# Giving back the slots of z earlier, and making the second mixing's pieces later

## The chip, the cores and the metric

The kernel runs on one core of one Trainium2 chip. The metric is the device time of one execution in microseconds, as a median of several runs; lower is better. Times inside an execution come from one profiled execution, counted from the start of its span. TensorE (PE in the rows; PEld is its weight load) multiplies into banks of PSUM, VectorE (DVE) and ScalarE (ACT) do the elementwise work, GpSimd (POOL) does small arithmetic and issues stores, and SyncE (SP) issues nearly all loads. Each of these works through its own queue in order.

## The reference

The program applies four layers to x, a float32 array of 2048 rows by 512 columns. Layers 0 and 2 mix, layers 1 and 3 are a gated feed-forward with 1792 hidden columns; the weights of the two of each kind are the same.

```python
def _A_ref(x, dft_seq_re, dft_seq_im, dft_hid_re, dft_hid_im):
    a = jnp.einsum("bsd,ed->bse", x, dft_hid_re)
    b = jnp.einsum("bsd,ed->bse", x, dft_hid_im)
    return jnp.einsum("ts,bse->bte", dft_seq_re, a) - jnp.einsum("ts,bse->bte", dft_seq_im, b)

def _B_ref(x, w_gate, w_up, w_down):
    return (_gelu(x @ w_gate) * (x @ w_up)) @ w_down

x = x + _A_ref(_layernorm(x), ...)
x = x + _B_ref(_layernorm(x), ...)
x = x + _A_ref(_layernorm(x), ...)
x = x + _B_ref(_layernorm(x), ...)
```

## The kernel before

**Numbers.** Every float32 operand is split into a high part (a rounding copy on ScalarE, L156) and a low part (a subtraction on VectorE, L158). A product is then three matmuls, high x high, high x low and low x high (`mm3`, L213 to L215), each 128x128 by 128x512. All of TensorE's real work runs through these three lines.

**Seven products in place of eight.** Both kinds of layer cut their matrix products into 2x2 blocks and use a scheme with seven block products. The names are those of the blocks of the weight and of the other operand: A11 with B11, A12 with B21, S1 with T1, S2 with T2, S3 with T3, S4 with B22, A22 with T4. S and T are sums and differences of blocks.

**Slots.** On-chip tiles of 128x512 float32 come from 98 numbered slots. `sb.get` takes the first number from the list of free ones, `sb.put` appends to its end, so the list is first in, first out. A slot may be handed out, in the program's text, while an earlier instruction that reads it has not yet run; the instruction that writes it next then waits for that reader. Which slot a load gets therefore decides what it waits for. The framework puts the instructions of each engine in order with a planning model of its own, so loads that have a free slot can be queued ahead of loads that stand earlier in the program's text.

**A feed-forward half.** `geglu(w, layer)` handles half w (1024 rows) of layer 1 or 3. Its normed rows, called z, lie transposed and split in `blocks`: 7 names x 2 chunks of 128, each a high and a low slot. Fourteen passes `up(n)`, n from 0 to 13, make the hidden values. Each pass runs the seven block products of `product(n, ps, an, bn, ...)` in this order: S2, S1, the next pass's A11 (`first(n + 1)`), S3, S4, the next pass's A12 (`second(n + 1)`), A22. A weight piece is given back behind its product, and the same piece for pass n + 2 is loaded from DRAM (`wb`, L1235). Even passes are followed by the gelu (L1245), odd ones by the multiplication with the gelu's result (L1261). The z blocks are read in all fourteen passes; they are given back in one loop behind the last (L1588).

**Beside the passes.** The down projection uses the same scheme over pairs of hidden blocks. Its A11 and A12 products run beside the passes (`beside`, one of six matmuls in each pass from n = 1); the other five names run behind the passes as a list of late products. Their weight pieces (`wc`) come through one stream of loads, issued on SP some items ahead (`take`, `load_next`, L333). In the second half of layer 1 the queue of steps also loads x again and makes the norm's terms for the next mixing (L241, L614 to L619, L640).

**The list `spare`.** In the second half of layer 1 (w = 1) a list of small jobs is laid out at L1386 to L1391. Four jobs make pieces of the hidden weights for two blocks of the second mixing: load a raw block (L1155 to L1157), four sums on VectorE, seven splits or half splits, and stores to DRAM (`wq`, L1182 and L1185, from POOL). Two jobs make summed blocks of the sequence weights: four loads (L1206), four sums, four stores (`ws`, L1216). Ahead of each job's work stands the load of the next one, and between them LET empty entries. `beside_mix(n)` takes one entry from the list each time it is called, which is six times in a pass, five of them through `beside_next`. It begins at pass n = 1 in layer 1. What the jobs make is read in layer 2, by SP loads from 1047 us on for `wq`. In layer 3 the same list holds products left over from layer 2, and is taken from in every pass.

Of the kernel before, what the change touches and what calls it, by code (L numbers as in the profile page):

```python
# [18 lines left out]
NF = F // P  # L19
# [24 lines left out]
MIXED = 4  # L44
PAIRED = {2: (2, 3)}
LATER = 3
LET = 5
SUMMED = 2
DOWN_RUNS = ((0,0,0,0),(4,4,4,0),(4,4,4,0),2)

# [2 lines left out]
def fnet_geglu(ctx: ExitStack, tc: tile.TileContext, x_in, ws, wh, wgu, wdn, wdc, whc, out):  # L53
# [86 lines left out]
    sb = Slots(slots, "s", NSLOT)  # L140
# [70 lines left out]
    def mm3(ps, a, b, start, stop):  # L211
        (ah, al), (bh, bl) = a, b
        nc.tensor.matmul(ps, ah, bh, start=start, stop=False, skip_group_check=True)  # L213
        nc.tensor.matmul(ps, ah, bl, start=False, stop=False, skip_group_check=True)  # L214
        newest["PE"] = nc.tensor.matmul(ps, al, bh, start=False, stop=stop, skip_group_check=True)  # L215
# [349 lines left out]
    def step():  # L565
        if queue:
            run = queue.pop(0)
            if run is not None:
                run()
        steps_done[0] += 1  # L570
        if slow and steps_done[0] % pace[0] == 0:
            slow.pop(0)()
# [129 lines left out]
    blocks = {}  # L702
# [98 lines left out]
    spare = []  # L801
# [429 lines left out]
    def piece_load(n, i):  # L1231
        tiles = [sb.get(F32R) for _ in range(2 if i < 3 else 1)]
        for k, t in enumerate(tiles):
            at = i * 1024 + k * 512
            nc.sync.dma_start(f32(t), wblocks[n][:, at:at + 512])  # L1235
        piece_here(n, i, tiles)
# [13 lines left out]
    def geglu(w, layer):  # L1250
# [43 lines left out]
        def product(n, ps, an, bn, start, stop):  # L1294
            step()
            hi, lo = wparts[n][an]
            for c in range(2):
                cut = slice(c * P, (c + 1) * P)
                mm3(ps, (hi[:, cut], lo[:, cut]), blocks[bn, c], start and c == 0, stop and c == 1)
            if an in ends:  # L1300
                i = ends[an]
                sb.put(*wparts[n][i])
                if not making and n + 2 < NF:
                    piece_load(n + 2, i)

        def first(n):
            if n < NF:
                chain[n] = ps8.get()
                product(n, chain[n], "A11", "B11", True, True)
                c11[n] = ps8.get()  # L1310
                seed(c11[n], chain[n])

        def second(n):
            if n < NF:
                ps = c11.pop(n)
                product(n, ps, "A12", "B21", False, True)
                finished(n, 0, 0, ps)
                ps8.put(ps)

        def beside_mix(n):  # L1320
            run = spare.pop(0) if spare and (layer > 1 or n >= 1) else None
            if run:
                run()

        def beside_next(n, down):
            beside_mix(n)
            next(down, None)

        def up(n):
# [4 lines left out]
            if n > 2 or w:  # L1334
                for _ in range(DOWN_RUNS[3]):
                    run = down_making.pop(0) if down_making else None
                    if run:
                        run()
            product(n, chain[n], "S2", "T2", False, True)
            u[n] = copied(chain[n])  # L1340
            down = beside(n)
# [4 lines left out]
            beside_next(n, down)  # L1346
            first(n + 1)
            beside_mix(n)
            product(n, chain[n], "S3", "T3", False, True)
            v = w4.pop(n)  # L1350
# [35 lines left out]
        if layer == 1 and w and PAIRED:  # L1386
# [3 lines left out]
            for n, (_, runs) in enumerate(jobs):  # L1390
                spare.extend([load for load, _ in jobs[n + 1:n + 2]] + [None] * LET + runs)  # L1391

# [189 lines left out]
        for n in range(NF):  # L1582
# [2 lines left out]
                    slow.pop(0)()  # L1585
                queue.extend(ahead_of_all)
            up(n)
        for bc in list(blocks):  # L1588
            sb.put(*blocks.pop(bc))
        if w == 0:  # L1590
            while slow:
                slow.pop(0)()
# [121 lines left out]
    for layer in range(4):  # L1714
        if layer % 2 == 0:
            mix(layer)
        else:
            for w in range(NB // 2):
                geglu(w, layer)
# [47 lines left out]
```

## Time and profile before

| | |
|---|---|
| median of three runs | 1598.59 us (1598.47, 1598.59 and 1994.72) |
| profiled execution | 1598.53 us, of which its span is 1596.8 us |
| TensorE busy | 1589.0 us of the span |
| VectorE, ScalarE, GpSimd busy | 1177.1, 890.3, 292.4 us |
| DMA | 431.75 MB, a mean of 270 GB/s |

A matmul's end is modelled in these records, so the busy share of TensorE tells where it had nothing to do, and the count of matmuls in a stretch tells how fast it went. A row of a list of waits gives who waited for what, then the total, the number of times and the longest, in us. The granted clock (PEclk) is a share of full speed. A DMA share of 1.0 is all 16 engines of the core busy; a little more than 1 can come out, since a transfer is booked in the stretch in which it starts. A group row ends with busy time and the mean of one instruction in ns, then the idle time of the engine just before and what ended it.

### The profile page before, as it was taken

The page shows a single profiled execution, that of the slowest core. Times are in us where ns is not written, and L with a number is a line of the kernel's source. Part 1 is how long each engine was busy: PE and PEld are TensorE (multiplying, and loading weights), DVE is VectorE, ACT ScalarE, POOL GpSimd, SP SyncE. Part 2 cuts the span into 40 slices and gives each one's busy share as a digit, 9 for nine tenths or more (in the row PEclk, how much of TensorE's full clock was granted, in tenths as well). Part 3 has the DMA queues.
Part 4 walks back from the last instruction along what each step waited for, and adds up shares of the span by engine and source line. Part 5 has one row for each costly group of instructions (what it writes and reads, how often), then busy time and mean ns, then how long its engine had stood idle before and what let it go on. Part 6 is the DMA issues. An engine that isn't in the chain of part 4 may idle for free.

```text
span 1596.8 us, 22853 instructions
## 1 busy us (share of the span) xinstructions
PE 1589.0 (100%) x6984; PEld 1309.6 (82%) x6984; DVE 1177.1 (74%) x2042; ACT 890.3 (56%) x1731; POOL 292.4 (18%) x493
## 2 busy tenths in 40 slices
PE   9999999999999999999999999999999999999998
PEld 6888888888888888888888888888888888888887
DVE  7997878888689794665879877777895557744573
ACT  8955465754767553565657545556452565333460
POOL 4112121251456101330030000011301000000000
PEclk9999999999999999999999999999999999999999
DMA  9878888996998999996895776877978958995445
GB/s 355 296 263 301 301 303 285 347 319 200 308 368 316 295 311 292 355 367 207 314 302 192 264 249 212 271 243 251 257 258 286 278 200 257 300 291 169 131 145 158
DMA packets 249434, 431.75 MB, mean 270 GB/s; under 512 B 29344, under 2 KB 74656, under 8 KB 248288
## 3 DMA queue, kind: packets, MB, share of 16 engines
q1 hardware_dynamic: 220464, 340.36, 65.9%
q0 software_dynamic: 26160, 87.84, 15.4%
q10 hardware_dynamic: 2688, 2.10, 0.5%
q8 instruction: 55, 0.90, 0.2%
q14 instruction: 67, 0.55, 0.1%
HBM read 344.46 MB, written 85.72 MB: 269 GB/s over the span
## 4 chain that ended last, share of the span: by engine, by line
PE 90%; issue 4%; DMA 3%; POOL 1%; ACT 1%; DVE 1%; SPq 0%; POOLq 0%; ACTq 0%; DVEq 0%
PE p L213 30%; PE p L214 30%; PE p L215 30%; DMA s<-t 1%; DMA s<-ws 1%; DMA s<-wc 1%; PE p L991 1%; DMA s<-x 1%; DMA xwide<-t 0%; POOL rstd L617 0%; ACT s L156 0%; DMA s<-wgu 0%; POOL wb L319 0%; DVE s L158 0%; POOL s L736 0%
## 5 line engine op out<-in xcount | busy, mean ns | idle before, releaser
L214 PE MATMUL p<-s,s 128*128 128x512 f32 x2312 | 896.8, 389 | 0.0
L215 PE MATMUL p<-s,s 128*128 128x512 f32 x2312 | 891.4, 389 | 0.0
L213 PE MATMUL p<-s,s 128*128 128x512 f32 x2312 | 858.4, 389 | 1.2 <-DMA s<-wc 0.9
L156 ACT ACTIVATE s<-s 128x512 fp32r<-128x512 f32 (+1 forms) x859 | 481.7, 607 | 259.5 <-DVE s L189 56.9
L158 DVE TENSOR_TENSOR s<-s,s 128x512 fp32r<-128x512 f32 (+1 forms) x859 | 539.0, 662 | 104.5 <-ACT s L156 91.6
L213 PEld LDWEIGHTS p<-s,s 128*128 128x128 f32 x2312 | 433.8, 188 | 93.2 <-DMA s<-wc 1.3
L214 PEld LDWEIGHTS p<-s,s 128*128 128x128 f32 x2312 | 434.0, 188 | 90.6 <-DVE s L158 0.4
L215 PEld LDWEIGHTS p<-s,s 128*128 128x128 f32 x2312 | 433.9, 188 | 90.5 <-DMA s<-wb 0.2
L193 DVE TENSOR_TENSOR s<-s,p 128x512 f32<-128x512 f32 x199 | 134.6, 683 | 166.1 <-PE p L215 137.8
L189 DVE TENSOR_TENSOR s<-s,s 128x512 f32<-128x512 f32 (+1 forms) x415 | 244.6, 610 | 3.5 <-DMA s<-ws 1.1
L200 ACT ACTIVATE s<-p 128x512 f32<-128x512 f32 x232 | 134.2, 593 | 124.8 <-PE p L215 121.5
L1245 ACT ACTIVATE s<-s 128x512 f32<-128x512 f32 x84 | 52.7, 628 | 41.0 <-DVE s L193 40.0
L617 POOL TENSOR_SCALAR rstd<-rstd 128x1 f32<-128x1 f32 x40 | 23.4, 586 | 239.9 <-ACT s L616 231.7
L1245 ACT ACTIVATE s<-p 128x512 f32<-128x512 f32 x28 | 16.7, 598 | 83.7 <-PE p L215 73.5
L319 POOL DMA_DIRECT2D wb<-s x84 | 46.2, 552 | 92.1 <-ACT s L156 69.8
L1261 DVE TENSOR_TENSOR s<-s,p 128x512 f32<-128x512 f32 x56 | 38.3, 684 | 23.0 <-PE p L215 23.0
L640 ACT ACTIVATE s<-s,shift,rstd 128x512 f32<-128x512 f32 x59 | 47.4, 811 | 10.6 <-DMA s<-x 4.9
L158 DVE TENSOR_TENSOR s<-xwide,s 128x512 fp32r<-128x512 f32 (+1 forms) x49 | 32.8, 677 | 25.8 <-ACT s L156 25.8
L196 DVE TENSOR_TENSOR s<-s,s 128x512 f32<-128x512 f32 (+1 forms) x73 | 44.1, 612 | 9.0 <-DMA s<-ws 7.1
L207 ACT ACTIVATE p<-p 128x512 f32<-128x512 f32 x56 | 32.7, 585 | 28.2 <-PE p L215 24.0
L722 DVE STREAM_TRANSPOSE wide<-s 128x512 f32<-128x512 f32 x31 | 21.9, 708 | 26.5 <-ACT s L640 21.9
L1182 POOL DMA_DIRECT2D wc<-s x42 | 30.6, 730 | 53.6 <-ACT s L156 36.1
(104 smaller groups left out, 619.1 us busy)
## 6 DMA issues: line engine op xcount, KB each, us to landing
s<-ws SPq DMA_DIRECT2D x406, 256.0 KB, 4.9
s<-wb SPq DMA_DIRECT2D x294, 256.0 KB, 5.2
s<-wc SPq DMA_DIRECT2D x182, 256.0 KB, 4.7
wb<-s POOLq DMA_DIRECT2D x98, 256.0 KB, 5.5
s<-wh SPq DMA_DIRECT2D x84, 256.0 KB, 5.4
s<-x SPq DMA_DIRECT2D x53, 256.0 KB, 5.4
wc<-s POOLq DMA_DIRECT2D x49, 256.0 KB, 5.4
xwide<-ws SPq DMA_DIRECT2D x36, 256.0 KB, 5.3
```

Of the source, the lines that this page charges most:

```text
L156: newest["ACT"] = nc.scalar.activation(hi, src, AF.Copy)
L158: newest["DVE"] = nc.vector.tensor_tensor(lo, src, f32(hi), op=ALU.subtract)
L189: nc.vector.tensor_tensor(out, a, b, op=ALU.subtract)
L193: bank_read["DVE"] = nc.vector.tensor_tensor(out, a, b, op=ALU.add)
L196: nc.vector.tensor_tensor(out, a, b, op=ALU.add)
L200: bank_read["ACT"] = nc.scalar.activation(v, src, AF.Copy)
L213: nc.tensor.matmul(ps, ah, bh, start=start, stop=False, skip_group_check=True)
L214: nc.tensor.matmul(ps, ah, bl, start=False, stop=False, skip_group_check=True)
L215: newest["PE"] = nc.tensor.matmul(ps, al, bh, start=False, stop=stop, skip_group_check=True)
L319: nc.gpsimd.dma_start(a, f32(t))
L640: nc.scalar.activation(z, x, AF.Identity, bias=shift, scale=rstd)
L1245: nc.scalar.activation(t, g, AF.Gelu_apprx_tanh)
```

## The change

Three edits. First, in the last pass a product gives the z blocks that it has read back at once, and the loop behind the passes goes. This holds for all four halves. Second, the empty entries between a job's load and its work go from five to four. Third, in layer 1 the list is taken from only from n = 3 on. The entries are otherwise the same, in the same order.

```diff
-LET = 5
+LET = 4
...
             for c in range(2):
                 cut = slice(c * P, (c + 1) * P)
                 mm3(ps, (hi[:, cut], lo[:, cut]), blocks[bn, c], start and c == 0, stop and c == 1)
+            if n == NF - 1:
+                for c in range(2):
+                    sb.put(*blocks.pop((bn, c)))
             if an in ends:
                 i = ends[an]
                 sb.put(*wparts[n][i])
...
         def beside_mix(n):
-            run = spare.pop(0) if spare and (layer > 1 or n >= 1) else None
+            run = spare.pop(0) if spare and (layer > 1 or n >= 3) else None
             if run:
                 run()
...
             up(n)
-        for bc in list(blocks):
-            sb.put(*blocks.pop(bc))
         if w == 0:
             while slow:
                 slow.pop(0)()
```

## The prediction

> **What bounds the kernel now.** I read three views: the page's first part, the busy time in stretches of 100 us (after the times: busy us of each engine with its instructions, TensorE's granted clock, the DMA engines' busy share and GB/s), and the list of what TensorE waited for (total, times, longest).
>
> ```profile
> span 1596.8 us, 22853 instructions
> PE 1589.0 (100%) x6984; PEld 1309.6 (82%) x6984; DVE 1177.1 (74%) x2042; ACT 890.3 (56%) x1731; POOL 292.4 (18%) x493
> ```
> ```profile
> core 0: us, PE busy (x) PEld busy (x) DVE busy (x) ACT busy (x) POOL busy (x), PEclk, DMA share, GB/s
> 600.00:700.00 100.00, 100.00 (x443) 82.81 (x442) 55.78 (x95) 51.39 (x111) 29.28 (x47) 1.00 1.04 332
> 700.00:800.00 100.00, 99.15 (x437) 81.74 (x437) 73.28 (x122) 61.86 (x119) 9.40 (x14) 1.00 0.80 280
> 1100.00:1200.00 100.00, 99.78 (x440) 82.02 (x440) 91.78 (x153) 52.54 (x97) 18.09 (x33) 1.00 0.84 256
> 1200.00:1300.00 100.00, 100.00 (x442) 82.54 (x441) 54.27 (x83) 49.63 (x106) 11.33 (x23) 1.00 0.84 255
> ```
> ```profile
> PE p L1673 <- POOL ident masks.py:199: 1.4, 1, 1.4
> PE p L213 <- DMA s<-wc: 0.9, 1, 0.9
> PE p L991 <- ACT s L640: 0.6, 1, 0.6
> PE p L991 <- ACT s L638: 0.3, 1, 0.3
> PE p L213 <- ACT p L207: 0.2, 1, 0.2
> ```
>
> TensorE is the bound almost everywhere. A stretch that it fills holds 443 matmuls in 100 us, 226 ns each. The profile finds only five waits on it. L1673 and L991 belong to the opening, before anything that the diff touches. What the change could take away is the other two: 0.9 us for a load of a down weight (`wc`), and 0.2 us for a seeded bank. So **the ceiling of any gain is 1.1 us**, 0.07% of the time. The busy time leaves out only what the records cannot show: a few stretches count 442 instead of 443, 0.2 us each.
>
> The 0.9 us lies in the part that the diff touches, the second half of layer 1. The chain of waits and the timeline around it:
>
> ```profile
> 761.16 5.35 DMA s<-wc
> 766.56 0.50 PE p L213
> ```
> ```profile
> 754.82 4.66 SPq L333 DMA_DIRECT2D s<-wc  x7
> ...
> 760.50 1.67 SPq L333 DMA_DIRECT2D s<-wc  x3
> ...
> 761.94 0.68 DVE L1261 TENSOR_TENSOR s<-s,p 128x512 f32<-128x512 f32 x1
> ```
>
> The load that TensorE waits for is issued at 761.16 us and takes 5.35 us. L1261 at 761.94 multiplies the last product of the fourteenth pass, so this is the seam between the passes and the late down products, just where the blocks of z go out of use. Ten loads of `wc` stand close together on SP. Why were they not issued earlier? The queue's own waits, and the traffic in that stretch:
>
> ```profile
> SPq L333 <- PE p L215: 16.8, 19, 5.2
> ```
> ```profile
> 735.00:747.00 12.00, 12.00 (x55) 9.94 (x54) 7.14 (x11) 6.82 (x12) 0.00 (x0) 1.00 0.40 116
> 747.00:762.00 15.00, 15.00 (x68) 12.43 (x67) 9.41 (x18) 12.18 (x24) 0.00 (x0) 1.00 0.74 251
> 762.00:772.00 10.00, 9.15 (x41) 7.21 (x40) 8.94 (x17) 7.88 (x17) 0.00 (x0) 1.00 1.05 390
> ```
>
> Between 735 and 783 us SP stood 16.8 us on slots whose last reader was a matmul, while the DMA engines were 0.40 and then 0.74 busy. Afterwards the transfers come in one burst at 1.05. The loads were short of free slots, not of bandwidth.
>
> **Part 1: blocks of z given back behind their last product.** No instruction is added or taken away. For the fourteenth pass of each half, 7 names x 2 chunks x 2 tiles = 28 of the 98 slots go back one product at a time (B11 and B21 already while the thirteenth ends), instead of together behind the pass. The list of free slots is first in, first out, so a longer list hands out slots whose last reader is further back. In the seam above this should let the `wc` loads go in the stretch with share 0.40. Price: at best the whole 0.9 us. TensorE was busy 9.15 of the 10.00 us of 762 to 772, so I put it at -0.85. At worst every slot number from there on is dealt anew, and a load stands as long as the longest slot wait above, 5.2 us, with all of it on TensorE. I take -0.85, since that is the row of this very place; -1.1 and +5.2 stay as ends. The other three halves show no wait of TensorE at their seams, so they give 0.
>
> **Part 2: the jobs start two passes later and stand closer.** The list `spare` makes pieces of the second mixing's hidden weights (`wq`, four jobs) and summed blocks (`ws`, two jobs). It had 3 + 4x11 + 7 + 6 = 60 entries. With LET 4 it has 3 + 4x10 + 6 + 5 = 54. Each pass takes six. Counting passes from 0, the old list ran from pass 1 to the last call of pass 10; the new one runs from pass 3 to the last call of pass 11, of the 66 calls that are left. The start moves by two passes, the end by one. What moves, and what it moves past, two passes to a row (an L1261 that reads a bank ends each odd pass: pass 1 at 625.96, pass 11 at 734.92):
>
> ```profile
> 626.00:648.00 22.00, 22.00 (x99) 18.22 (x98) 14.08 (x26) 11.77 (x24) 5.77 (x9) 1.00 1.09 289
> ...
> 670.00:692.00 22.00, 22.00 (x99) 18.22 (x98) 12.94 (x24) 12.35 (x29) 6.53 (x11) 1.00 1.04 387
> ...
> 714.00:735.00 21.00, 21.00 (x95) 17.38 (x94) 14.72 (x25) 10.31 (x20) 5.47 (x8) 1.00 0.84 298
> ```
> ```profile
> 625.96 0.69 DVE L1261 TENSOR_TENSOR s<-s,p 128x512 f32<-128x512 f32 x1 [0.38 <-PE p L215]
> ...
> 734.92 0.69 DVE L1261 TENSOR_TENSOR s<-s,p 128x512 f32<-128x512 f32 x1 [0.24 <-PE p L215]
> ```
> ```profile
> L158 DVE TENSOR_TENSOR s<-s,s 128x512 fp32r<-128x512 f32 x42 | 28.7, 689 | 14.2 <-ACT s L156 12.5 <-PE p L214 0.7 <-ACT s L616 0.6
> L189 DVE TENSOR_TENSOR s<-s,s 128x512 f32<-128x512 f32 x31 | 20.7, 687 | 0.4
> L189 DVE TENSOR_TENSOR s<-s,s 128x256 f32<-128x256 f32 x16 | 6.3, 418 | 0.0
> L158 DVE TENSOR_TENSOR s<-s,s 128x256 fp32r<-128x256 f32 x8 | 3.3, 424 | 5.5 <-ACT s L156 5.4
> ```
>
> A `wq` job costs VectorE 4 x 0.418 for the sums and 3 x 0.689 + 0.424 for the splits, 4.2 us; a `ws` job 4 x 0.687 = 2.75 us. The total is unchanged. Counted by the list, both `ws` jobs now fall into passes 10 and 11, where one of them was: 14.72 + 2.75 + about 0.5 for a last split = 18.0 us of 21.0. Passes 2 and 3 lose a job: 14.08 - 4.2 = 9.9 of 22. So VectorE has room in every row, ScalarE more. I cost the work at 0; its cover is the 3.0 us that VectorE keeps idle in passes 10 and 11, and if it fails, a `ws` job's 2.75 us is what a split behind it is late by.
>
> Its transfers go with it: 20 loads on SP (3 for a `wq` job, 4 for a `ws` job) and 36 stores on POOL (7 and 4). Their first and last rows, and those of what they move past:
>
> ```profile
> L333 SPq DMA_DIRECT2D s<-wq x28: 319/320/423, 1047.0 to 1185.1; - x28
> L1182 POOL DMA_DIRECT2D wq<-s x24: 722/727/780, 630.9 to 698.4; - x24
> ```
> ```profile
> 722.84 0.54 POOL L1216 DMA_DIRECT2D ws<-s  x1 [0.18 <-issue]
> ```
> ```profile
> 715.06 1.40 POOL L617 TENSOR_SCALAR rstd<-rstd 128x1 f32<-128x1 f32 x1 [0.82 <-ACT s L616]
> ...
> 749.57 1.52 ACT L640 ACTIVATE s<-s,shift,rstd 128x512 f32<-128x512 f32 x2 [0.86 <-DMA s<-x]
> ```
>
> The first reader of `wq` is at 1047.0; a last store 11 us later than 722.84 is still 313 us early. On POOL the stores share a strict order with the terms of the next layer's norm: L617 at 715.06 may now stand behind a store that waits for ScalarE. It is first used at 749.57, 34 us later, against a move of at most two passes, 22 us. On SP the jobs' loads pass among the weight pieces `wb`, which are asked for two passes ahead, so a few places in the queue cost nothing. The stretch in which the DMA engines are full (1.09, 1.04) loses a job at its front; the emptier row, 0.84, gains one. Sum for part 2: 0.
>
> **Sum.** 1598.53 us for the profiled execution (span 1596.8 and 1.7 around it, 0.06 below the median 1598.59) - 0.85 + 0 = **1597.7 us**.
>
> What a longer stall would do to the clock can be seen behind the last matmul:
>
> ```profile
> 1592.50:1597.00 4.50, 0.00 (x0) 0.00 (x0) 0.62 (x1) 0.00 (x0) 0.00 (x0) 0.78 0.41 157
> ```
>
> In 4.5 us without a matmul the granted clock falls to a mean of 0.78, while the row with the 0.85 us stall kept 1.00; so short waits cost their own length. "TensorE: Matmul & The Clock Gate" of the Trainium skill (Part 1) has the clock halved after an idle window of about 3.4 us, and full again after a busy one of the same length; both rows agree. By that rule, a stall of over 3.4 us would cost an estimated 1.7 us more than itself.
>
> **The rivals.**
> *The wait stays.* The given-back slots join the end of the list, and a load in the seam may still draw an old one whose reader is late; or the stall moves to another load of the burst. For it: the burst row at 1.05 shows that once loads bunch, each lands 5.4 us later, whatever slot it has. Against: the 0.40 row in front. Time: 1598.53, or up to one more such wait, 1599.4. This is also the case in which the change does not do what it says.
>
> *VectorE is late in passes 10 and 11* (slower). Both `ws` jobs, 5.5 us, stand there in VectorE's queue, next to the splits that the late down products need and that are prepared ahead in these passes. Behind VectorE's queue then stand those splits, and TensorE behind them. It decides once more than the 3.0 us of idle time is used up, or a needed split is queued right behind a job. Price: one job, 2.75 us, to both, 5.5: 1598.53 + 2.75 = 1601.3 to 1604.0, less 0.85 if the seam's wait goes: 1600.4 at the low end. Against it: 18.0 of 21.0 fits, and the row 1100 to 1200 shows VectorE 92% busy with TensorE losing 0.2 us.
>
> *The interval of the matmuls shrinks* (faster by more). If the 226 ns were held up by neighbours' traffic, a calmer stretch could run faster, down to a weight load's 1309.6/6984 = 188 ns. At the very most that is 1598.5 - 6984 x 0.038 = 1333. "Trainium Kernel Development and Optimization" (Best Practices) in the Trainium skill says to judge the distance to the limit by weight loads' busy share, here 82%, not by matmuls', which fits such a hope. But the rows of 735 to 747 (share 0.40, 55 records in 12 us) and 670 to 692 (1.04, 99 in 22) have the same rate, so nothing here moves it.
>
> **How the numbers follow.** Forecast 0.50 (1597.4 to 1598.1); the wait stays 0.28 (to 1599.4); VectorE late 0.18 (1600.4 to 1604.0); slower by over 2%, 32 us, which takes the same lateness of 3.6 us in each of the nine passes with jobs, 0.02; matmul interval 0.01; 0.01 unexplained. The low end is the ceiling, 1598.53 - 1.1, less 0.7 for three such stretches of 442: 1596.7. The high end takes in VectorE's case up to one job and half of the other, 1602.7, and so leaves out less than 1 in 10. 2% is about what a measurement of this kernel can tell from no change: faster 0.01, within 0.97, slower 0.02.
>
> **What would show it.** Right: no wait of TensorE for `wc` near 766 us; SP's waits on matmuls between 735 and 783 well below 16.8 us; a higher DMA share than 0.40 in 735 to 747; the first `wq` store about 20 us later than 630.9, the last `ws` store about 11 us later than 722.84, both with 99 matmul records to 22 us around them. Wrong: a new wait of TensorE behind L158 near 714 to 762, or behind a load in the mixing that follows, where the slots are dealt anew. The forecast fails if such waits sum to more than 1 us.

## The result, and the profile after

The changed kernel takes 1605.63 us in the median; the kernel before, measured beside it, 1598.95 us, 6.7 us less. The ratio of the fast runs, which leaves out one run of the kernel before of 1994.72 us, is 1.0047, with a 95% interval of 1.0035 to 1.0058. So the changed kernel is slower by some 7.5 us (5.6 to 9.3). That is far below 2%, but clear, and outside the forecast's range. The profiled execution took 1604.69 us, its span is 1602.9 us, 6.1 us more than before. The page's first part, and what TensorE waited for:

```profile
span 1602.9 us, 22828 instructions
PE 1592.7 (99%) x6984; PEld 1311.6 (82%) x6984; DVE 1175.6 (73%) x2042; ACT 888.9 (55%) x1731; POOL 296.2 (18%) x493
```
```profile
PE p L213 <- ACT s L200: 3.3, 2, 2.0
PE p L1674 <- POOL ident masks.py:199: 1.4, 1, 1.4
PE p L213 <- ACT s L156: 1.0, 2, 0.7
PE p L213 <- ACT p L207: 0.2, 1, 0.2
```

The work is the same, and the 0.9 us for `wc` is gone, as forecast. New are two waits on L200, ScalarE's copy of a finished product out of PSUM, and two on L156, its rounding copies. They sum to 4.3 us. Where they lie shows in the busy time of the changed kernel in stretches of 100 us:

```profile
600.00:700.00 100.00, 97.99 (x425) 80.61 (x425) 48.34 (x82) 45.45 (x98) 21.26 (x35) 0.98 1.01 298
700.00:800.00 100.00, 100.00 (x443) 82.78 (x442) 76.17 (x130) 66.07 (x130) 15.03 (x25) 1.00 0.90 309
800.00:900.00 100.00, 98.99 (x435) 80.91 (x434) 85.64 (x182) 63.46 (x123) 22.21 (x36) 1.00 0.74 245
1200.00:1300.00 100.00, 98.66 (x435) 81.28 (x434) 52.09 (x80) 48.35 (x104) 11.32 (x23) 1.00 0.87 260
```
The row of the kernel before for 800 to 900 was not shown yet:
```profile
800.00:900.00 100.00, 100.00 (x442) 82.55 (x442) 86.06 (x182) 66.82 (x130) 21.40 (x36) 1.00 0.77 255
```

Counted in matmuls: 443 to 425, 437 to 443, 442 to 435, 442 to 435. That is 18 lost, 6 won, 7 and 7 lost, 26 in all; at 226 ns each, 5.9 of the span's 6.1 us. The 18 are the main item, 4.1 us in one place. Here is ScalarE's timeline there in the changed kernel (start, duration, and in brackets the idle time before with what ended it):

```profile
640.42 0.63 ACT L614 ACTIVATE s<-s 128x512 f32<-128x512 f32 x1 [4.59 <-DMA s<-x]
...
642.13 1.06 ACT L200 ACTIVATE s<-p 128x512 f32<-128x512 f32 x2
```

The same stretch of ScalarE in the kernel before:

```profile
637.79 0.59 ACT L200 ACTIVATE s<-p 128x512 f32<-128x512 f32 x1
...
639.30 0.60 ACT L200 ACTIVATE s<-p 128x512 f32<-128x512 f32 x1
639.78 0.42 ACT L156 ACTIVATE s<-s 128x256 fp32r<-128x256 f32 x1
642.06 0.63 ACT L614 ACTIVATE s<-s 128x512 f32<-128x512 f32 x1 [1.85 <-DMA s<-x]
```

L614 is the first sum of a row tile of x, for the next mixing's norm. Nobody needs it soon. Before, it stood in ScalarE's queue behind the L200 copies and the splits of the jobs (L156); it waited 1.85 us for its tile, and nobody behind it was in a hurry. With the job's splits gone from these passes, the framework's plan has L614 ahead of L200. The tile itself comes no later than before (L614 runs at 640.42 us in place of 642.06); what is new is the order. (The steps with L614 are bound to come behind the instruction of ScalarE that stands last in the program's text when they are laid out, at L163. As I read the code, that was a split of a job before, and is an earlier instruction now.) ScalarE works in order: it stands 4.59 us on a load, and the finished products stay in PSUM behind it; below, this is called the knot. The chain of waits of the changed kernel (start, length, what) leads from the load over L200 to TensorE, and tells how long the load took:

```profile
631.54 8.85 DMA s<-x
...
642.22 0.98 ACT s L200 x2
643.20 0.04 issue
643.25 0.50 PE p L213
...
644.95 0.43 PE p L213
...
648.54 0.23 PE p L213
```

And the wait costs more than itself. In fine stretches of the changed kernel, the granted clock falls behind it:

```profile
642.00:644.00 2.00, 0.76 (x3) 0.67 (x4) 0.00 (x0) 2.00 (x7) 0.74 (x2) 1.00 1.03 213
644.00:646.00 2.00, 2.00 (x7) 1.55 (x6) 0.91 (x2) 0.87 (x2) 0.00 (x0) 0.68 0.23 75
646.00:648.00 2.00, 2.00 (x6) 1.58 (x5) 0.93 (x2) 0.00 (x0) 0.00 (x0) 0.50 1.14 289
648.00:650.00 2.00, 2.00 (x10) 1.58 (x10) 2.00 (x6) 0.60 (x1) 0.00 (x0) 0.97 0.97 291
```

A mean of 0.68 over 2 us is 1.28 us at one half; with 2.0 and 0.12 us in the next rows, the half clock lasted 3.4 us, and the matmuls took 0.43 in place of 0.23 us. So the place lost 2.0 us idle, 1.7 us by the half clock and some 0.3 by the slow first matmul: 4.0 of the 4.1 us.

The gap of 1.3 us in 1200 to 1300 has the same form, in layer 3: there too L614 stands ahead of L200, in both kernels, and it stood longer on its load in the changed one (before, then after, each ScalarE's timeline):

```profile
1229.01 0.63 ACT L614 ACTIVATE s<-s 128x512 f32<-128x512 f32 x1 [2.66 <-DMA s<-x]
```
```profile
1235.34 0.63 ACT L614 ACTIVATE s<-s 128x512 f32<-128x512 f32 x1 [4.22 <-DMA s<-x]
```

### The profile page after: what moved, and what is told of

It reads as the page before. It is cut to its first block, busy times and chain, and to the rows that moved or that the text cites. A ratio compares the mean times of both kernels' runs of the same rounds, so it can differ in the third digit from the quotient of the medians.

```text
span 1602.9 us, 22828 instructions
## 1 busy us (share of the span) xinstructions
PE 1592.7 (99%) x6984; PEld 1311.6 (82%) x6984; DVE 1175.6 (73%) x2042; ACT 888.9 (55%) x1731; POOL 296.2 (18%) x493
## 4 chain that ended last, share of the span: by engine, by line
PE 93%; DMA 2%; issue 2%; ACT 1%; POOL 1%; DVE 0%; POOLq 0%; DVEq 0%; ACTq 0%; SPq 0%
PE p L213 31%; PE p L214 31%; PE p L215 31%; DMA s<-t 1%; DMA s<-x 1%; PE p L991 1%; POOL rstd L617 0%; PE p L1674 0%; ACT s L156 0%; DMA s<-wb 0%; POOL s L736 0%; DMA xwide<-ws 0%; ACT xwide L200 0%; ACT s L614 0%; DVE s L193 0%
## 5 line engine op out<-in xcount | busy, mean ns | idle before, releaser
L215 PE MATMUL p<-s,s 128*128 128x512 f32 x2312 | 892.4, 389 | 0.0
L156 ACT ACTIVATE s<-s 128x512 fp32r<-128x512 f32 (+1 forms) x859 | 482.1, 607 | 265.9 <-DVE s L189 66.9
L158 DVE TENSOR_TENSOR s<-s,s 128x512 fp32r<-128x512 f32 (+1 forms) x859 | 539.2, 663 | 113.3 <-ACT s L156 89.1
L215 PEld LDWEIGHTS p<-s,s 128*128 128x128 f32 x2312 | 434.4, 188 | 90.2
L200 ACT ACTIVATE s<-p 128x512 f32<-128x512 f32 x232 | 133.7, 592 | 121.4 <-PE p L215 112.9
L1245 ACT ACTIVATE s<-s 128x512 f32<-128x512 f32 x84 | 52.6, 628 | 41.6 <-DVE s L193 41.4
L1245 ACT ACTIVATE s<-p 128x512 f32<-128x512 f32 x28 | 16.8, 598 | 82.4 <-PE p L215 80.6
L158 DVE TENSOR_TENSOR s<-xwide,s 128x512 fp32r<-128x512 f32 (+1 forms) x49 | 32.9, 679 | 23.1 <-ACT s L156 23.1
L207 ACT ACTIVATE p<-p 128x512 f32<-128x512 f32 x56 | 32.7, 585 | 24.1 <-PE p L215 24.0
L614 ACT ACTIVATE s<-s 128x512 f32<-128x512 f32 x36 | 22.4, 623 | 33.5 <-PE p L214 17.2
```

The costliest lines, as they stand in the source:

```text
L156: newest["ACT"] = nc.scalar.activation(hi, src, AF.Copy)
L158: newest["DVE"] = nc.vector.tensor_tensor(lo, src, f32(hi), op=ALU.subtract)
L200: bank_read["ACT"] = nc.scalar.activation(v, src, AF.Copy)
L1245: nc.scalar.activation(t, g, AF.Gelu_apprx_tanh)
```

## The experiments

The theory (Q in the expectations): edit 3 costs time, because it takes the jobs' ScalarE work out of passes 2 and 3, so that L614 comes to stand ahead of L200 and waits there for its load. Edits 1 and 2 alone were expected to cost nothing. The rivals: edit 1 has dealt the slots anew, so that the load of x comes later (S); or the jobs' late end takes VectorE's time from the down products, as the prediction's own rival had it (R). All ratios are against the kernel before on the same chip, with their 95% interval; 0.0010 is 1.6 us. A ratio need not be that of the two medians; here they differ by up to 0.0009.

### Each edit alone

**Edit 1 alone: the slots of z given back early.**
```diff
+            if n == NF - 1:
+                for c in range(2):
+                    sb.put(*blocks.pop((bn, c)))
...
-        for bc in list(blocks):
-            sb.put(*blocks.pop(bc))
```


> Only the first edit: z's blocks go back behind their last product; LET stays 5 and the list starts at pass 1. Theory Q (the late start changes ScalarE's order: the norm's sum L614 is queued ahead of two evacuations L200 and waits there for its own load of x): ScalarE's order round the first L614 is that of before, so no wait of TensorE for L200 near 641 us; time 1597.7 to 1599, the 0.85 us wait for wc at 766 gone. Theory S (slots dealt anew make the loads of x late): the waits of after for L200 near 641 and 1235 us are here too, and the time is 1603 to 1606.

Measured: 1.0002 (0.9992 to 1.0011). The new row in its list of TensorE's waits:
```profile
PE p L213 <- ACT s L200: 1.0, 1, 1.0
```
The wait for `wc` is gone, and a wait of 1.0 us behind L200 at 1230 us has come for it. In the seam, SP's waits on L215 fall from 16.8 to 14.9 us, and the DMA share of 735 to 747 rises from 0.40 to 0.46. So the edit does what it says, in a small measure, and gives nothing. No wait for L200 stands near 641 us, so theory S falls for that place. The wait near 1230 us is not this edit's own: eleven of the thirteen changed builds here have 0.3 to 1.3 us there, with edit 1 and without it.

**Edit 2 alone: four empty entries in place of five.**
```diff
-LET = 5
+LET = 4
```


> Only LET 4, the list still starts at pass 1 and the blocks go back behind the loop. Theory Q: ScalarE has the first L614 behind the copies' first pair and job splits between, so no 2 us wait near 641; time within 1.5 us of before, 1597.5 to 1600.5. Theory S says nothing of this edit beyond the dealing of slots, which also changes here: a wait at 1235 us and 1600 to 1603.

Measured: 1.0037 (1.0027 to 1.0047), 5.9 us, where none was expected: a miss. The profiled execution (1609.35 us) is its longest, so its waits are larger than the ratio asks for. ScalarE's timeline and the stretches around it:
```profile
638.36 0.42 ACT L156 ACTIVATE s<-s 128x256 fp32r<-128x256 f32 x1
647.56 0.63 ACT L614 ACTIVATE s<-s 128x512 f32<-128x512 f32 x1 [8.78 <-DMA s<-x]
...
648.71 0.57 ACT L200 ACTIVATE s<-p 128x512 f32<-128x512 f32 x1
```
```profile
640.00:644.00 4.00, 2.50 (x12) 1.73 (x10) 0.00 (x0) 0.00 (x0) 0.33 (x1) 1.00 1.12 199
644.00:648.00 4.00, 0.00 (x0) 0.00 (x0) 0.00 (x0) 0.44 (x1) 0.00 (x0) 0.61 0.98 366
648.00:652.00 4.00, 2.66 (x6) 2.16 (x7) 1.38 (x2) 2.88 (x9) 0.74 (x2) 0.50 1.15 199
652.00:656.00 4.00, 4.00 (x12) 3.12 (x11) 3.70 (x8) 0.60 (x1) 0.00 (x0) 0.61 1.12 221
```
The same knot, drawn tighter: L614 stands 8.78 us with L200 behind it, TensorE 6.8 us, and the half clock lasts 3.12 + 4.0 + 3.12 = 10.2 us, some 4.5 us of them while TensorE still stood. No work has left these passes here. With LET 4 the job's last split comes one entry sooner, at 638.36 us in place of 639.78. L614, which as I read the code is bound behind it, then stands ahead of the third L200, which ran at 639.30 us before and now runs at 648.71. The `wc` wait stays here, 1.2 us.

**Edit 3 alone: the list is taken from only from the fourth pass on.**
```diff
-            run = spare.pop(0) if spare and (layer > 1 or n >= 1) else None
+            run = spare.pop(0) if spare and (layer > 1 or n >= 3) else None
```


> Only the third edit: the list starts at pass 3. Theory Q: ScalarE's first L614 stands ahead of two L200 as in after; TensorE waits about 2.0 us for L200 near 641 us, its clock is halved for about 4 us behind it, 18 matmul records are missing in 600 to 700, together 4.1 us: time 1602.5 to 1604 before other waits. Theory S: without the slots given back the wait is not there; 1598.5 to 1600.

Measured: 1.0037 (1.0024 to 1.0049). In its profile, the shortest of its executions (1602.41 us), L614 again stands ahead of two L200 and holds TensorE for 0.9 us; further waits of 0.9 us (L158, at 768) and 0.3 and 0.7 us (L156, at 890 and 892) come later:
```profile
638.71 0.63 ACT L614 ACTIVATE s<-s 128x512 f32<-128x512 f32 x1 [3.46 <-DMA s<-wc]
```
The row names a load of `wc`, but in the chain of waits the load of x, 630.23 to 638.62 us, stands right ahead of L614. This profile shows 5 matmuls lost in 600 to 700 and 7 in 800 to 900, with the clock at 1.00; 18 and a half clock were expected in the first place. The median lies 2.9 us above it, and no profile shows where those were lost.

So edits 2 and 3 each cost about 0.4% alone. Edit 1 costs nothing, and what it wins in its place is lost in layer 3. The two costs don't add up in the changed kernel (1.0047). Both pass through the same place, which I take for the reason.

### Taking away what L614 waits for

**The changed kernel, the first tile loaded one step earlier.** The steps that make the norm's terms load their first tile themselves. Here an empty step ahead of them loads it; everything else is as changed.
```diff
-        if i == 0:
-            fresh["terms"] = x_load(layer, 0)
...
-            slow.extend([lambda: None] * 4 + [paced(lambda k=k: terms_ahead(layer + 1, k, NK)) for k in range(NK)])
+            slow.extend([lambda: None] * 3 + [lambda: fresh.update(terms=x_load(layer + 1, 0))])
+            slow.extend(paced(lambda k=k: terms_ahead(layer + 1, k, NK)) for k in range(NK))
```


> All three edits, and the first x tile of the norm's terms is loaded one entry of the slow list (one pass, 10.9 us) earlier than the terms that use it, in place of an empty entry. ScalarE's order is that of after. Theory Q: L614 finds its tile, waits for nothing and the wait for L200 near 641 with its halved clock goes; 4.1 us less than after, 1601 to 1602. Rival D (ScalarE is late there for another reason, or the stretch is bound by the slow transfers of xwide): the wait stays and the time with it, 1605.

Measured: 1.0009 (1.0000 to 1.0018), against 1.0047 for the changed kernel without it (by the medians 2.7 us above the kernel before, against 6.7). ScalarE's timeline and the stretch:
```profile
635.10 0.62 ACT L614 ACTIVATE s<-s 128x512 f32<-128x512 f32 x1
```
```profile
600.00:700.00 100.00, 100.00 (x443) 82.84 (x442) 52.28 (x89) 49.01 (x106) 25.07 (x41) 1.00 1.03 312
```
L614 still stands ahead of L200, but no longer waits, and the stretch has its 443 matmuls. In this place the wait on the load was the cause, not the order alone.

**The changed kernel, the terms one step later.** This alters where L614 stands, and leaves its load where it is used.
```diff
-            slow.extend([lambda: None] * 4 + [paced(lambda k=k: terms_ahead(layer + 1, k, NK)) for k in range(NK)])
+            slow.extend([lambda: None] * 5 + [paced(lambda k=k: terms_ahead(layer + 1, k, NK)) for k in range(NK)])
```


> All three edits, with one more empty entry ahead of the norm's terms, so that the first terms with their own load come one pass (10.9 us) later; the load is not earlier than its use. In ScalarE's order the first L614 now stands behind a pair of evacuations L200 and splits L156. Theory Q (it is the order, not the load, that costs): no wait for L200 near 641, 1600.5 to 1602.5, as with the early load. If the late load by itself were the cost, L614 would hold TensorE again near 652 us and the time stay at 1604 to 1606.

Measured: 1.0013 (1.0004 to 1.0023). The load of x is issued at 642.98, and ScalarE's three L200 stand at 636.83 and 638.42 with no L614 ahead of them; no wait is left there. Two different edits that break the knot, one at the load and one at the order, each give back 5.4 to 6.1 of the 7.5 us by the ratios.

**The same early load beside each edit alone**, to see whether it makes each of them harmless, and what it does by itself. Edit 3, then edit 2, then edit 1, each with the diff of the early load above:

> Only the start at pass 3, with the first x tile one pass earlier. Theory Q takes the wait near 641 away: 3 us or so less than the start alone (1605.3). Theory R (a second cost of the late start: the jobs' work on VectorE moves to 735 to 762 us and stands before the full stretch of VectorE to 900): the waits for L156 or L158 at 880 to 900 stay, and the time is 1601 to 1602.5, above before. Without R it is 1599 to 1600.

> Only LET 4, with the first x tile of the norm's terms loaded one pass earlier. ScalarE's order is that of the run with only LET 4, where L614 waited 8.8 us for its tile and TensorE 6.8 us for L200 near 649 us. Theory Q: with the tile there in time the wait and the halved clock go; 1599 to 1601. If LET costs its time elsewhere, the time stays at 1604 to 1609.

> Only z's slots given back early, with the first x tile one pass earlier; ScalarE's order is that of before. Theory Q: nothing to gain near 641, since L614 stands behind the evacuations; no wait for wc at 766. 1598 to 1600, ratio 0.999 to 1.001. A clear gain or loss here would mean that the early load does something by itself, and would spoil the reading of the other runs with it.

Measured: with edit 3, 1.0013 (1.0003 to 1.0022) in place of 1.0037. Its waits on L156 near 890 us, 1.0 us, stayed, as theory R forecast. With edit 2, 1.0023 (1.0012 to 1.0035) in place of 1.0037, a median of 1603.62 us and so above the 1599 to 1601 expected: the first knot is gone, but a later L614 now makes one, 1.4 us of TensorE at 663.8. With edit 1, 1.0009 (0.9996 to 1.0021) in place of 1.0002, so the early load is worth nothing where there is no knot. The later L614, in ScalarE's timeline of edit 2 with the early load:
```profile
661.04 0.63 ACT L614 ACTIVATE s<-s 128x512 f32<-128x512 f32 x1 [3.98 <-DMA s<-whc]
```
This row names a load of a job. The tile of x, issued at 652.25 us, took 8.7 us and landed at the same time, 661.0.

**Edit 2, every tile of the terms loaded two steps ahead.**
```diff
-LET = 5
+LET = 4
...
-        if i == 0:
-            fresh["terms"] = x_load(layer, 0)
-        x, junk = fresh.pop("terms"), sb.get()
-        if i + 1 < n:
-            fresh["terms"] = x_load(layer, i + 1)
+        x, junk = fresh.pop(("terms", i)), sb.get()
+        if i + 2 < n:
+            fresh["terms", i + 2] = x_load(layer, i + 2)
...
-            slow.extend([lambda: None] * 4 + [paced(lambda k=k: terms_ahead(layer + 1, k, NK)) for k in range(NK)])
+            slow.extend([lambda: None] * 2 + [lambda k=k: fresh.update({("terms", k): x_load(layer + 1, k)}) for k in range(2)])
+            slow.extend(paced(lambda k=k: terms_ahead(layer + 1, k, NK)) for k in range(NK))
```


> Only LET 4, with every x tile of the norm's terms loaded two passes ahead (with one pass ahead, L614 still held TensorE 1.4 us at 664 us, where LET 4 puts it right ahead of another pair of L200). Theory Q: no wait of TensorE for L200 is left between 600 and 700, 443 matmul records there, and the time falls from 1603.6 to 1599.5 to 1601. If it stays at 1603 or above, LET 4 has a second cost.

Measured: 1.0022 (1.0010 to 1.0034), a miss. No L200 wait is left in 600 to 700, but a load of a hidden weight piece is late there instead, 1.8 us at 660.9, after 10.57 us on its way. The row in its list of TensorE's waits:
```profile
PE p L215 <- DMA s<-wb: 1.8, 1, 1.8
```
So beside L614 some 3.5 us are left (1.6 to 5.4). Whether that is a second cost of edit 2, by the jobs' transfers standing closer, or one of the early loads, by the slots that they hold, no run tells apart.

### What is left: the late end, the late start

The changed kernel with the early load, and edit 3 with it, keep 1.4 and 2.1 us, by intervals of 0 to 3.5 us. I took the jobs' late end to be the cause: in the changed kernel the last `ws` work comes among the splits for the down products.

**The kernel before, only the end moved**: six empty entries ahead of the load of the last `ws` job. The sums of both `ws` jobs stand behind that load, so both come one pass later.
```diff
             for n, (_, runs) in enumerate(jobs):
+                spare.extend([None] * (6 if n == ND else 0))
```


> Before, with six empty entries ahead of the last ws job's load: the list starts at pass 1 with LET 5 as before, but the two ws jobs end one pass later, at the end of pass 11, as in after. ScalarE's order round the first four L614 is that of before. Theory R (the jobs' later end puts their VectorE work before the full stretch to 900 us): new waits of TensorE between 760 and 900 for L156 or L158, 1 to 2.5 us together, 1600.5 to 1602.5. If R is wrong, the time is before's, 1599 to 1600, and the second cost hangs on the start.

Measured: 0.9993 (0.9983 to 1.0002). VectorE's busy time in the seam, before and with the late end, rises from 16.55 to 19.64 of 27.00 us, and TensorE keeps its 121 matmuls:
```profile
735.00:762.00 27.00, 27.00 (x121) 22.36 (x120) 16.55 (x29) 19.00 (x35) 0.00 (x0) 1.00 0.59 191
```
```profile
735.00:762.00 27.00, 27.00 (x121) 22.36 (x120) 19.64 (x34) 19.26 (x36) 1.08 (x2) 1.00 0.75 252
```
The late end alone costs nothing. That theory fell.

**The late start with the end in its old place**: edit 3, LET 3, every tile two steps ahead.
```diff
-LET = 5
+LET = 3
...
-            run = spare.pop(0) if spare and (layer > 1 or n >= 1) else None
+            run = spare.pop(0) if spare and (layer > 1 or n >= 3) else None
```
and the early loads as in the diff of edit 2 above.

> The list starts at pass 3 with LET 3, 48 entries, so it ends with pass 10 as before; every x tile of the terms is loaded two passes ahead, and the blocks of z go back behind the loop. Theory Q: no wait near 641. Theory R: with the end of before the waits of 333 and 670 ns at 889 to 892 and of 0.86 us at 768 go, and the time is 1599 to 1600.5. If R is wrong, those waits stay and the time is 1601 to 1602.5.

Measured: 1.0002 (0.9993 to 1.0012), with 443 matmuls in 600 to 700 and in 700 to 800. The wait at 768 is gone. Near 890 its profile, the longest of ten executions, still has waits of TensorE, now on VectorE:
```profile
PE p L214 <- DVE s L158: 1.4, 2, 0.9
```
So that part of the expectation missed, while the time came as expected. The late start costs nothing clear either, once no load holds ScalarE and the end stays.

**Edit 1 with the late end**, the start in its old place: the diff of edit 1 and that of the moved end together.

> Edit 1 alone plus six empty entries ahead of the last ws job, so that the jobs begin in pass 1 as before and end in pass 11 as after the change. What is told apart: whether the rest of about 1 to 2 us that the builds with a start at pass 3 keep is due to edit 1 and the late end together. If each part stays harmless together as it was alone (ratios 1.0002 and 0.9993), no wait of over 0.3 us between 620 and 790 us, and a time of 1598 to 1600 us. If the two together are the rest, a TensorE wait of 0.7 us or more stands between 760 and 895 us as in the builds with the late start, and the time is 1600.5 to 1602 us. This is also the one candidate left to beat the kernel before: it holds both parts that cost nothing alone. It beats it only if the wait behind L200 near 1231 us, 1.0 to 1.1 us in both parts alone, is not dealt again: then 1597 to 1598 us.

Measured: 1.0003 (0.9994 to 1.0012). The list of waits holds 1.3 us behind L200 at 1230.8 and 0.2 us behind L207, and nothing between 620 and 895 us. So the rest isn't those two together. In the times it appears where a late start and a late end meet, 1.4 to 2.1 us. Their profiles have waits of 0.3 to 2.1 us between 766 and 895 us, whose place and releaser vary from build to build. But such waits near 890 stand in two other builds too: 1.4 us with the end in its old place, 1.1 us with edit 1 and the early load. What the rest comes from is **open**; no run isolates it, and some of it may be the early load itself, whose 1.0009 beside edit 1 is not clear of 1. No build here is clearly faster than the kernel before.

## Why the prediction was wrong

**The bound and the ceiling** held: TensorE was the bound, and no edit won more than the 1.1 us.

**Part 1** (-0.85) was right in its place and wrong in its sum. The wait at 766 went. In the changed kernel SP's waits on L215 between 735 and 783 fell from 16.8 to 11.6 us, and the DMA share of 735 to 747 rose from 0.40 to 0.69 (SP's waits, then the stretch):
```profile
SPq L333 <- PE p L215: 11.6, 11, 4.4
```
```profile
735.00:747.00 12.00, 12.00 (x54) 9.95 (x53) 10.38 (x19) 5.70 (x11) 2.17 (x4) 1.00 0.69 219
```
Most of that is not part 1's doing: with edit 1 alone the two are 14.9 us and 0.46. With the late end alone, and no edit 1, they are 9.2 us and 0.62, and the wait for `wc` is gone there too. So moving the jobs does at least as much in this seam as giving the slots back. "The other three halves show no wait of TensorE at their seams, so they give 0" failed. Edit 1 alone has 1.0 us at 1230, which takes the gain back; the late end alone has 1.1 us there, so any new dealing of the slots may do it, which was not tested. Before, L614 stood there for 2.66 us on its tile with no wait of TensorE behind it: cover that was nearly used up, and that the prediction did not look for.

**Part 2** (0) is the step that failed, by some 7 us (the changed kernel's 1.0047 against 1.0002 with edit 1 alone). "VectorE has room in every row, ScalarE more" is true, and beside the point: it judged ScalarE by its busy time, 11.77 of 22 us, and VectorE, POOL and SP by what stands in their queues. ScalarE's own queue was left out. Passes 2 and 3 came out emptier, as worked out (VectorE 6.67 of 22 us, where 9.9 were expected), and this was the harm in the main: the work that was taken away had held a waiting instruction back, which then cost 4.0 us in one place. The two-pass rows of the changed kernel:
```profile
626.00:648.00 22.00, 19.99 (x82) 16.08 (x81) 6.67 (x10) 8.66 (x18) 0.74 (x2) 0.93 1.03 212
...
714.00:735.00 21.00, 21.00 (x94) 17.37 (x93) 14.27 (x23) 9.86 (x21) 5.76 (x10) 1.00 1.00 361
```

**"Short waits cost their own length"** failed. It rested on a wait of 0.85 us; one of 2.0 us was followed by a half clock that cost nearly as much again. That "both rows agree" was a misreading too: in the kernel before, in stretches of 1 us, the clock is 1.00 up to 1595.00 us and 0.51 from there, 3.0 us after the last matmul began at 1592.01. That is less than the 3.4 us of idle time that the prediction took for the limit.

**The rivals.** The wait for `wc` did not stay, and the interval of the matmuls did not shrink (a stretch that TensorE fills still holds 443 in 100 us). VectorE in passes 10 and 11 was not late: the row of 714 to 735 has it at 14.27 of 21.0 us, and part of the work came a pass later, with 18.86 of 27.00 us in 735 to 762. TensorE was full in both, and the late end alone cost nothing. The range's upper side was there for this rival alone, and fell 3 us short of the median. "A new wait of TensorE behind L158 near 714 to 762, or behind a load in the mixing that follows" named the wrong engine and the wrong place for the changed kernel: L200 at 643 and 1236 us, L156 at 891 and 894.

**What would show it.** The first `wq` store came 26 us later, at 656.8; about 20 were forecast, and some 4 are the time lost at 643. The last `ws` store came 22 us later, 4 of them the same; 11 were forecast, counted by the list. With the late end alone it came 15 us later. The stores waited for VectorE's sums, so VectorE was behind the list; why was not tried. Around the first store there were to be 99 matmuls in 22 us, as before; the row above has 82. GpSimd's timeline of the changed kernel:
```profile
656.78 2.25 POOL L1182 DMA_DIRECT2D wq<-s  x3 [13.62 <-ACT s L156]
...
744.92 0.54 POOL L1216 DMA_DIRECT2D ws<-s  x1 [1.87 <-DVE s L189]
```

## What to carry to other kernels

When work is moved out of a stretch, or only one entry sooner as in edit 2, look at each engine that did it for what moves up in its queue: an instruction that waits for a load may come to stand ahead of the one that TensorE needs. A row with an idle time on a DMA ahead of a harmless instruction (here L614, 1.85 and 2.66 us) marks such a spot in the profile of before, even where no engine suffers from it yet. A load that is used in the step that issues it is the thing to mend: moving it one step ahead gave back most of the loss.

## What the runs showed of the hardware

Idle time alone does not decide the half clock. The wait of 2.0 us at 643 was followed by 3.4 us at one half; in the changed kernel with the early load, a wait of 2.1 us at 891.7 was followed by none (its stretches):
```profile
890.00:892.00 2.00, 0.28 (x1) 0.28 (x2) 1.97 (x4) 2.00 (x5) 0.00 (x0) 1.00 0.61 246
892.00:894.00 2.00, 2.00 (x10) 1.62 (x10) 2.00 (x5) 2.00 (x5) 0.00 (x0) 1.00 0.50 166
```
It is the same behind the last matmul of a program: with edit 3 alone the half clock came 2.5 us after that matmul began, in the kernel before 3.0 us after, and in the changed kernel not within the 4.6 us to the end. "TensorE: Matmul & The Clock Gate" of the Trainium skill (Part 1) has the half clock after at least one idle window of about 3.4 us; here it came after less, and the measurement decides. The same part says that the window, 3413 ns long, is free-running, so that the moment at which the clock changes depends on where in the window the first matmul lands. The lengths agree, 3.4 us and 10.2 us being one and three windows; where the windows begin no run here shows.

A load of one tile of x, 256 KB, took 8.85 us in the changed kernel (631.54 to 640.39), where the median of such loads is 5.3 us (the row of the DMA issues below). In that time the DMA share was above 1 at only 181 to 233 GB/s, while the stretch of 670 to 692 in the kernel before moved 387 at 1.04. The end of the load:
```profile
638.00:640.00 2.00, 2.00 (x11) 1.65 (x10) 0.00 (x0) 0.00 (x0) 0.00 (x0) 1.00 1.15 181
```
```profile
s<-x SPq DMA_DIRECT2D x53, 256.0 KB, 5.3
```
A low rate is not needed for a slow load: with edit 2 and the early load, the tile issued at 652.25 us took 8.7 us while the engines moved 400 GB/s. What makes these loads slow wasn't tried.
